# Gate and up of every f tile as one 2x2 block product, in an adaLN block with linear attention and a bilinear FFN

## The chip, the cores and the metric

One core of a Trainium2 chip. The metric is the device time of one execution in microseconds; a kernel's time is the median of its runs. All data is float32; matrix products run on float32r halves (below).

## The reference

```python
mod = (silu(c) @ w_mod).reshape(c.shape[0], 6, 1, -1)
sa, ca, ga, sb, cb, gb = (mod[:, i] for i in range(6))
h = layernorm(x) * (1 + ca) + sa
q, k, v = heads(h @ wqkv)                       # 32 heads of 16
phi = lambda t: where(t > 0, t + 1, exp(t)) + 1e-6
kv  = einsum("bhsd,bhse->bhde", phi(k), v)
z   = einsum("bhsd->bhd", phi(k))
o   = einsum("bhqd,bhde->bhqe", phi(q), kv) / (einsum("bhqd,bhd->bhq", phi(q), z)[..., None] + 1e-6)
x = x + ga * (merge(o) @ wo)
h = layernorm(x) * (1 + cb) + sb
x = x + gb * (((h @ w_gate) * (h @ w_up)) @ w_down)
```

x is 1 x 2048 x 512, w_gate and w_up 512 x 1376, w_down 1376 x 512, wqkv 512 x 1536, wo 512 x 512.

## The kernel before

**Tiles.** The 2048 tokens are 4 chunks (`ch`) of 4 token tiles (`j`) of 128; token tile `i` is `4 ch + j`. D = 512 is 4 blocks of 128 (`k`). F = 1376 is 11 f tiles, ten of 128 columns and a last one of 96.

**Float32 by halves.** Every operand of a product is split into a rounded half h (ScalarE copy, `split`, L183) and the rest l (a subtraction, L184, on VectorE or GpSimd). A product is three matmuls: h h, h l, l h.

**Order.** The program is recorded in the order of the source, and each engine runs its own part of it in that order; engines wait for each other by semaphores alone. SBUF tiles come from one pool of 99 buffers; PSUM is two pools of four banks, `ps_acc` (`acc`) and `ps_w` (`bank`).

**Stages.**
1. Layer norm of x, the modulation columns, k and the sums over tokens (`t_tile`, `z_add`), 4 chunks; q of tiles 0 to 10 among and after them.
2. The weights of kv folded into wo: `kvps` (products of `wv` and `tt`, where `tt` are the split sums of `tacc`), `w_out`, `wp`.
3. For each token tile a y step: `turn_a` transposes phi(q) (4 matmuls, L579), `turn_h` and `turn_l` (L583, L587) make its halves, `y_a` multiplies by `wp` (12 matmuls, L609), `y_seed` (L600) puts x into the bank beforehand, `y_b` (L614) copies the sum back to x and takes the statistics of layer norm 2. Before it, phi(q) is divided by its denominator: `den_p` (L487, a product with z), `den_r` (L493, a sum over a head), `den_b` (L502, L503, an add and a reciprocal for a whole chunk), `den_c` (L510).
4. Layer norm 2 by chunks: `rstd_of` (a power on GpSimd, L236), `nmr_of`, `xhat` (L245, ScalarE), `transpose` (L252), `modulated` (L266 to L271; it also writes the result `f` to DRAM as `kept`).
5. The FFN. f tiles 8, 9 and 10 (`lone`) are computed plainly, chunk by chunk, and stand between the y steps: `gate_up(ch, f)` (L684 to L686; 24 matmuls) and `down` (L708 to L710). f tiles 0 to 7 are four `pairs`. For a pair and a side (two chunks, 0 and 1 or 2 and 3) gate is one 2x2 block product and up another: rows are the two chunks, columns the two f tiles, the inner dimension is cut into two halves of 256. Seven products in place of eight (`block`, L973; `times`, L936), with sums of left factors (`Left`: a11, s1, s2, a12, s3, a22, s4) and of weights (`Right`: b11, t1, t2, b21, t3, t4, b22; L909, L920, L923, L927, on GpSimd and ScalarE). A block is 7 x 6 = 42 matmuls on four banks (`abank` to `dbank`), and `down_pair` (L957 to L959; 24 matmuls) of the blocks before stands between its fifth and sixth product. `evac` (L671) adds to x.

The left factors of the second side are made early, in `steps` of a list that is worked off a few at a time (`trickle`, `some`), written to DRAM and read back (`fetch`) at the change of sides. In the order of the source:

```python
y_step(0, lambda: den_c(3), lambda: q_b(11))
y_step(1)
y_step(2, lambda: split_gu(f0, nc.gpsimd))
y_step(3, lambda: scale_down(f0), turn=False, seed=False)
ps12 = proj(12, wq)
...
g = gate_up(0, f0)
...
y_step(4, lambda: scale_down(f2), lambda: den_a(2, 1, on=nc.vector))
g = gate_up(0, f2)
```

Of the kernel before, what the change touches and what calls it, by code (L numbers as in the profile page):

```python
# [11 lines left out]
ALU = mybir.AluOpType  # L12
# [10 lines left out]
def tile_adaln_block(  # L23
# [25 lines left out]
    lone = list(range(8, NF))  # L49
    pairs = [(f, f + 1) for f in range(0, 8, 2)]  # L50
# [165 lines left out]
    class Norm:  # L216
        def __init__(self, tiles):
            self.tiles = tiles
            self.mv = T(small, "mv", (P, NJ, 2))
            self.n = [None] * NJ  # L220
            self.ps = [None] * KD
            self.t = [None] * KD
# [25 lines left out]
        def transpose(self, *ks):  # L248
            for k in ks:
                ps = bank()  # L250
# [253 lines left out]

    def den_c(*tiles):
# [24 lines left out]
    den_z()  # L530
    den_a(0, 0, 1, on=nc.vector)
# [17 lines left out]
    q_b(7)  # L549
    den_a(0, 2, on=nc.vector)  # L550
# [24 lines left out]
    def turn_a(i):  # L575
        tps[i] = bank()
        phi = phq.pop(i)
        for k in range(KD):
            nc.tensor.transpose(tps[i][:, k * P:(k + 1) * P], phi[:, k * P:(k + 1) * P], ident)  # L579
# [9 lines left out]
    def turn(i):  # L589
        turn_a(i)  # L590
        turn_h(i)
        turn_l(i)

    def y_seed(i, of=acc_bank):

        yps[i] = of()
        if of is bank:

            nc.tensor.matmul(yps[i], wp[0][0][:, :P], wp[0][0], start=True, stop=True)
        nc.scalar.activation(yps[i], xts[i // NJ][i % NJ], AF.Copy)  # L600

    def y_a(i):
        if i not in yps:
            y_seed(i)
        pq = pqs.pop(i)
        for k in range(KD):
            (ah, al), (bh, bl) = cut(pq, k * P, (k + 1) * P), wp[k]
            for x, y in ((ah, bh), (ah, bl), (al, bh)):
                nc.tensor.matmul(yps[i], x, y, start=False, stop=k == KD - 1 and x is al, skip_group_check=True)  # L609

    def y_b(i):
        ch, j = divmod(i, NJ)
        ps = yps.pop(i)
        nc.scalar.activation(xts[ch][j], ps, AF.Copy)  # L614
        norm2[ch].stats(j, of=ps)

    def y_step(i, *more, late=(), q=None, turn=True, seed=True):
# [3 lines left out]
        if turn and i + 1 < NT and i + 1 not in pqs:  # L621
            turn_a(i + 1)
        y_a(i)
        if i + 1 in tps:
            turn_h(i + 1)
            turn_l(i + 1)
        if i - 1 in yps:
# [3 lines left out]
        if seed and i + 1 < NT:  # L631
            y_seed(i + 1)
        for do in more:
            do()
        for do in late:
            do()

    norm2 = {}


    wf = {}

    raw_f = {}

    def load_ffn(f):
        f0, n = fts[f]
        raw_f[f] = (load(wg_v[:, :, f0:f0 + n], "raw"), load(wu_v[:, :, f0:f0 + n], "raw"),
                    load(w_down[f0:f0 + n, :], "raw"))

    def scale_down(f):  # L650
        d = raw_f[f][2]
        nc.vector.tensor_tensor(d, d, gb[:d.shape[0]], op=ALU.mult)

    def split_gu(f, low=None):
        n = fts[f][1]
        wf[f] = [split_raw(raw, (P, KD, n), low) for raw in raw_f[f][:2]]

    def split_down(f, low=None):
        wf[f].append(split_raw(raw_f.pop(f)[2], low=low))

    def split_ffn(f, low=None):
        split_gu(f, low)
        split_down(f, low)

    def prepare(f):
        return lambda: (scale_down(f), split_ffn(f))

    def evac(ch, dn, js=range(NJ), last=False):
        for j in js:
            xt = xts[ch][j]  # L670
            nc.vector.tensor_tensor(xt, dn[j], xt, op=ALU.add)  # L671
            if last:
                nc.sync.dma_start(ov[ch, j], xt)

    hs = {}

    def gate_up(ch, f):

        n = fts[f][1]
        gps, ups = bank(), bank()  # L680
        for w, ps in ((wf[f][0], gps), (wf[f][1], ups)):
            for k in range(KD):
                hh, hl = norm2[ch].t[k]
# [496 lines left out]
```

## Time and profile before

| | us |
|---|---|
| median of 3 runs | 575.12 |
| lowest, highest | 574.57, 575.14 |
| span of the profiled execution | 575.5 |
| TensorE busy in it | 566.6 (98%) |
| VectorE, ScalarE, GpSimd busy | 380.3, 288.2, 158.5 |

The profiled execution is one more execution of the same program. Its span is 0.36 us above the highest of the runs; the page has no other time for it, so what lies around the span can't be told from its own rows. Busy times of matmuls overlap: a matmul is listed with the time from its start to its end, and the next begins before that end.

### The profile page before, as it was taken

The page shows a single profiled execution, that of the slowest core. Times are in us where ns is not written, and L with a number is a line of the kernel's source. Part 1 is how long each engine was busy: PE and PEld are TensorE (multiplying, and loading weights), DVE is VectorE, ACT ScalarE, POOL GpSimd, SP SyncE. Part 2 cuts the span into 40 slices and gives each one's busy share as a digit, 9 for nine tenths or more (in the row PEclk, how much of TensorE's full clock was granted, in tenths as well). Part 3 has the DMA queues.
Part 4 walks back from the last instruction along what each step waited for, and adds up shares of the span by engine and source line. Part 5 has one row for each costly group of instructions (what it writes and reads, how often), then busy time and mean ns, then how long its engine had stood idle before and what let it go on. Part 6 is the DMA issues. An engine that isn't in the chain of part 4 may idle for free.

```text
span 575.5 us, 7302 instructions
## 1 busy us (share of the span) xinstructions
PE 566.6 (98%) x2587; PEld 463.7 (81%) x2587; DVE 380.3 (66%) x628; ACT 288.2 (50%) x503; POOL 158.5 (28%) x156
## 2 busy tenths in 40 slices
PE   7999999999999999999999999999999999999997
PEld 6778888888888778878878788888888888888885
DVE  6877868868768876656377755777865354545475
ACT  3585857546366535437365535363555343534430
POOL 2000000000011300000000244676755766574610
PEclk9799999999999999999999999999999999999999
DMA  8900213401401000101705113363489826210004
GB/s 280 373 5 2 73 62 102 132 0 43 108 1 41 35 1 36 38 0 60 233 2 182 38 37 118 102 184 110 148 280 359 263 76 191 56 55 2 0 1 146
DMA packets 46500, 57.17 MB, mean 99 GB/s; under 512 B 5152, under 2 KB 23584, under 8 KB 46464
## 3 DMA queue, kind: packets, MB, share of 16 engines
q1 hardware_dynamic: 46464, 56.71, 30.5%
q8 instruction: 20, 0.33, 0.3%
q14 instruction: 16, 0.13, 0.1%
HBM read 40.96 MB, written 15.73 MB: 99 GB/s over the span
## 4 chain that ended last, share of the span: by engine, by line
PE 92%; DVE 4%; DMA 2%; ACT 1%; issue 0%; POOL 0%; SPq 0%; ACTq 0%
PE bank L941 26%; PE acc L609 7%; PE bank L198 5%; PE bank L196 5%; PE acc L959 5%; PE bank L197 5%; PE acc L957 5%; PE acc L958 5%; PE bank L685 4%; PE bank L686 4%; PE bank L684 4%; PE acc L329 3%; PE acc L328 3%; PE acc L327 3%; PE acc L709 2%; PE acc L708 2%
## 5 line engine op out<-in xcount | busy, mean ns | idle before, releaser
L941 PE MATMUL bank<-h,w 128*128 128x512 f32 x672 | 155.4, 389 | 0.1
L941 PEld LDWEIGHTS bank<-h,w 128*128 128x128 f32 x672 | 126.1, 188 | 26.7 <-DMA h<-side_s 0.5
L184 POOL TENSOR_TENSOR w<-raw,w 128x512 fp32r<-128x512 f32 x22 | 31.7, 1462 | 118.4 <-DVE mv L228 87.5
L236 POOL TENSOR_TENSOR rstd<-ve,half 128x4 f32<-128x4 f32 (+1 forms) x9 | 9.3, 1038 | 169.4 <-DVE ve L235 165.0
L671 DVE TENSOR_TENSOR x<-acc,x 128x512 f32<-128x512 f32 x80 | 50.2, 679 | 3.5 <-PE acc L959 3.5
L927 POOL TENSOR_TENSOR w<-raw,w 128x256 fp32r<-128x256 f32 (+1 forms) x28 | 33.0, 1178 | 70.2 <-ACT w L920 70.2
L947 ACT ACTIVATE bank<-bank 128x512 f32<-128x512 f32 x32 | 18.6, 582 | 66.0 <-PE bank L941 66.0
L183 ACT ACTIVATE kh<-phi 128x512 fp32r<-128x512 f32 (+1 forms) x44 | 26.9, 628 | 47.2 <-DVE phi L693 33.9
L959 PE MATMUL acc<-w,kl 128*128 128x512 f32 x128 | 49.9, 390 | 0.0
L958 PE MATMUL acc<-w,kh 128*128 128x512 f32 x128 | 49.8, 389 | 0.0
L957 PE MATMUL acc<-w,kh 128*128 128x512 f32 x128 | 49.8, 389 | 0.0
L196 PE MATMUL bank<-w,h 128*128 128x512 f32 x112 | 44.9, 401 | 0.0
L198 PE MATMUL bank<-w,h 128*128 128x512 f32 x112 | 43.9, 392 | 0.0
L197 PE MATMUL bank<-w,h 128*128 128x512 f32 x112 | 43.6, 389 | 0.0
L1028 DVE TENSOR_TENSOR g<-bank,u 128x512 f32<-128x512 f32 x16 | 11.1, 692 | 45.5 <-PE bank L941 45.5
L184 DVE TENSOR_TENSOR kl<-phi,kh 128x512 fp32r<-128x512 f32 (+1 forms) x44 | 33.4, 771 | 9.6 <-ACT kh L183 8.8
L927 POOL TENSOR_TENSOR w<-t,w 128x512 fp32r<-128x512 f32 x28 | 38.8, 1386 | 0.0
L685 PE MATMUL bank<-h,w 128*128 128x512 f32 (+1 forms) x96 | 37.7, 393 | 0.3 <-DVE h L271 0.2
L684 PE MATMUL bank<-h,w 128*128 128x512 f32 (+1 forms) x96 | 37.8, 394 | 0.0
L686 PE MATMUL bank<-h,w 128*128 128x512 f32 (+1 forms) x96 | 37.6, 392 | 0.0
L609 PE MATMUL acc<-w,xh 128*128 128x512 f32 x112 | 35.5, 398 | 0.0
L245 ACT ACTIVATE n<-x,nmr,rstd 128x512 f32<-128x512 f32 x32 | 24.0, 804 | 22.4 <-DVE nmr L239 22.4
(172 smaller groups left out, 1193.7 us busy)
## 6 DMA issues: line engine op xcount, KB each, us to landing
raw<-in_w_mod_dram SPq DMA_DIRECT2D x24, 256.0 KB, 3.8
raw<-in_B_w_down_dram SPq DMA_DIRECT2D x18, 256.0 KB, 3.7
x<-in_A_x_dram SPq DMA_DIRECT2D x16, 256.0 KB, 5.4
kept<-f SPq DMA_DIRECT2D x16, 256.0 KB, 2.0
f<-kept SPq DMA_DIRECT2D x16, 256.0 KB, 4.7
raw<-in_B_w_gate_dram SPq DMA_DIRECT2D x32, 128.0 KB, 3.2
raw<-in_B_w_up_dram SPq DMA_DIRECT2D x32, 128.0 KB, 3.4
side_s<-h SPq DMA_DIRECT2D x16, 256.0 KB, 2.9
```

Of the source, the lines that this page charges most:

```text
L184: (low or nc.vector).tensor_tensor(l, src, f32(h), op=ALU.subtract)
L196: nc.tensor.matmul(ps, ah, bh, start=i == 0, stop=False)
L197: nc.tensor.matmul(ps, ah, bl, start=False, stop=False)
L198: nc.tensor.matmul(ps, al, bh, start=False, stop=i == n - 1)
L609: nc.tensor.matmul(yps[i], x, y, start=False, stop=k == KD - 1 and x is al, skip_group_check=True)
L684: nc.tensor.matmul(ps[:n], w[0][:, k], hh, start=k == 0, stop=False)
L685: nc.tensor.matmul(ps[:n], w[0][:, k], hl, start=False, stop=False)
L927: sub = lambda out, x, y: (on or nc.gpsimd).tensor_tensor(out, x, f32(y), op=ALU.subtract)
L941: mm = lambda x, y, **kw: nc.tensor.matmul(ps, x[:, k], y, skip_group_check=True, **kw)
L957: nc.tensor.matmul(dn[j], hh[:, a:b], dh, start=i == 0, stop=False)
L958: nc.tensor.matmul(dn[j], hh[:, a:b], dl, start=False, stop=False)
L959: nc.tensor.matmul(dn[j], hl[:, a:b], dh, start=False, stop=i == len(hs) - 1)
```

## The change

- There are no `lone` tiles, and `gate_up`, `split_gu`, `modulated` for layer norm 2 and their weights are gone. Each of the 11 f tiles is a block of its own, on each side: 22 blocks. The columns of its 2x2 product are gate and up of that f tile (`Right` loads both), so one block gives gate and up for two chunks, and their product: c11 and c12 for the first chunk, c22 and c21 for the second.
- `down` takes the f tiles in groups of two (the last of three), as `fillers` that lie between the fifth and the sixth product of later blocks; the last group's stand behind the last block.
- The y steps 0 to 11 stand in a row. Products q 12 to 15 lie in steps 4, 7, 9 and 11. y 12 to 15 lie inside blocks 0 to 2 (`early`), layer norm 2 of chunks 2 and 3 in blocks 0 to 5.
- Denominators: the product with z (`den_q`, from tile 4 on) is on GpSimd; sum, add and reciprocal are done tile by tile (`den_t`) on VectorE.
- Left factors of the first side are made from tiles that stay in SBUF (`plain`), all seven of them split; only chunks 2 and 3 go to DRAM. x of chunks 2 and 3 is loaded a second time (`reload_x`).
- A y product that no `y_seed` began opens its bank itself and is added to x on VectorE.

The core of the diff:

```diff
-    lone = list(range(8, NF))
-    pairs = [(f, f + 1) for f in range(0, 8, 2)]
...
+    def den_t(*tiles):
+        for i in tiles:
+            ch, j = divmod(i, NJ)
+            den_r(ch, j)
+            d = dens[ch][:, j]
+            nc.vector.tensor_tensor(d, d, den0, op=ALU.add)
+            nc.vector.reciprocal(d, d)
+
+    def den_q(*tiles):
+        for i in tiles:
+            den_p(*divmod(i, NJ))
...
     den_z()
+    den_p(1, 0, 1)
     den_a(0, 0, 1, on=nc.vector)
...
+    den_p(1, 2)
     den_a(0, 2, on=nc.vector)
...
+    def y_step(i, q=None, pe=(), after=(), pre=(), mid=()):
         if q is not None:
             ps = proj(q, wq)
+        if i + 1 < NT:
             turn_a(i + 1)
+        run(pre)
+        run(pe)
+        if i + 2 < NT:
+            den_c(i + 2)
         y_a(i)
+        if i + 1 < NT:
             turn_h(i + 1)
             turn_l(i + 1)
+        run(mid)
+        if i > 0:
             y_b(i - 1)
         if q is not None:
             q_a(q, ps)
+        if i + 1 < NT:
             y_seed(i + 1)
+        if q is not None:
+            q_b(q)
+        run(after)
...
+            for kh in range(2):
+                t = B("raw", (P, 2, KH, self.n))
+                for i, v in enumerate((wg_v, wu_v)):
+                    nc.sync.dma_start(t[:, i], v[:, kh * KH:(kh + 1) * KH, f0:f0 + self.n])
...
+        times(c, A["s3"], R["t3"], False)
+        u3 = B("u")
+        copy(u3[:n], c)
+        c22 = B("g")
+        nc.vector.tensor_tensor(c22[:n], d, u3[:n], op=ALU.add)
+        also("s3")
+        also("pe")
+        times(c, A["a22"], R["t4"], False)
+        also("mid")
+        times(d, A["s4"], R["b22"], False)
+        c12 = B("g")
+        def rest():
+            nc.vector.tensor_tensor(c12[:n], d, u2[:n], op=ALU.add)
+            product_of(0, g[:n], c12[:n])
+        product_of(1, c, c22[:n])
+        rest()
+        also("s4")
...
+    turn_a(0)
+    ps = proj(11, wq)
+    turn_h(0)
+    turn_l(0)
+    y_seed(0)
+    den_c(1)
+    q_a(11, ps)
+    q_b(10)
+    right_load(0)
+    right_load(1)
+    y_step(0, after=[lambda: q_b(11), lambda: den_q(7), lambda: den_t(4, 5), lambda: right_sums(0)])
+    y_step(1, after=[lambda: den_q(8), lambda: den_t(6, 7)])
+    y_step(2, after=[lambda: right_split(0), lambda: den_t(8)])
+    y_step(3, after=[lambda: n2[0].rstd_of(0, 3), lambda: den_q(9, 10)])
+    reload_x(8, 9, 10, 11)
+    y_step(4, q=12, pre=[lambda: n2[0].nmr_of(0, 3)], after=[lambda: n2[0].rstd_of(3, 4), lambda: n2[0].xhat(0, 1, 2), lambda: den_t(9), lambda: n2[0].nmr_of(3, 4), lambda: den_q(11)])
+    y_step(5, pre=[lambda: n2[0].xhat(3)], after=[lambda: den_t(10), lambda: den_q(12)])
+    y_step(6, pe=[lambda: ln2_turn(0, 0, 1)], after=[lambda: ln2_f(0, 0, 1), lambda: den_t(11)])
...
+    y_step(9, q=14, pre=[lambda: n2[1].xhat(3)], pe=[lambda: ln2_turn(1, 0, 2)], mid=[lambda: ln2_f(1, 0, 2)],
+           after=[lambda: [L[k].split("a11") for k in range(KH)], lambda: L[0].sum("s1"), lambda: den_t(13)])
+    y_step(10, pe=[lambda: ln2_turn(1, 1, 3)], mid=[lambda: ln2_f(1, 1, 3)],
+           after=[lambda: right_sums(1), lambda: den_q(14), lambda: L[1].sum("s1"), lambda: L[0].split("s1"), lambda: L[0].sum("s2")])
+    y_step(11, q=15, mid=[lambda: L[1].split("s1"), lambda: L[1].sum("s2")],
+           after=[lambda: L[0].split("s2"), lambda: L[0].split("a12"), lambda: den_t(14), lambda: n2[2].rstd_of(0, 3)])
+    L[0].sum("s3", "s4", on=nc.gpsimd)
+    y_b(11)
+    L[1].split("s2", "a12")
+    L[1].sum("s3", "s4")
...
+    groups = [[0, 1], [2, 3], [4, 5], [6, 7], [8, 9, 10]]
+    order = [(s, g, f) for s in range(2) for g in range(len(groups)) for f in groups[g]]
...
+    early = {
+        (0, "a11"): [lambda: y_a(12)],
+        (0, "s1"): [lambda: L[0].split("s3"), lambda: turned(13), lambda: ln2_r(2, 3, 4)],
+        (0, "s2"): [lambda: L[1].split("s3")],
+        (0, "s3"): [lambda: [L[k].split("a22") for k in range(KH)]],
+        (0, "pe"): [lambda: y_a(13), lambda: [L[k].split("s4") for k in range(KH)], lambda: y_b(12)],
+        (0, "mid"): [lambda: den_q(15), lambda: den_c(14), lambda: ln2_m(2), lambda: ln2_x(2, 0)],
+        (0, "s4"): [lambda: y_b(13), lambda: ln2_x(2, 1)],
+        (1, "s1"): [lambda: turned(14), lambda: ln2_x(2, 2)],
...
+    for n, (s, g, f) in enumerate(order):
...
+        if s == 0 and n > 5:
+            at["s1"].append(lambda: some(3))
+        if s == 0 and n >= 5:
+            at["s4"].append(lambda: some(3))
```

580 lines of the change are left out of this document (206 added, 374 removed).

## The prediction

> **What bounds the kernel now.** I read the page first, then the waits of TensorE, then the chain in order of time, and last the groups by form, the windows and the timelines around the part that changes.
>
> ```profile
> span 575.5 us, 7302 instructions
> PE 566.6 (98%) x2587; PEld 463.7 (81%) x2587; DVE 380.3 (66%) x628; ACT 288.2 (50%) x503; POOL 158.5 (28%) x156
> ...
> PEclk9799999999999999999999999999999999999999
> ```
> ```profile
> PE acc L143 <- DVE w L138: 2.0, 1, 2.0
> ...
> PE bank L579 <- DVE xl L587: 0.6, 2, 0.3
> ...
> PE bank L685 <- DVE h L271: 0.2, 1, 0.2
> ```
>
> TensorE works 566.6 of 575.5 us, and its waits after the first stage are 0.6 + 0.2 us. So time can be won only by taking matmuls away, and every wait that the new order makes is lost in full. What is one matmul worth? The groups say 389 ns each, but they overlap; the chain gives the distance:
>
> ```profile
> 377.74 9.52 PE bank L941 x42
> 392.70 9.52 PE bank L941 x42
> ```
> ```profile
> L941 PE MATMUL bank<-h,w 128*128 128x512 f32 x672 | 155.4, 389 | 0.1
> ...
> L684 PE MATMUL bank<-h,w 128*96 128x512 f32 x32 | 12.6, 393 | 0.0
> ```
>
> 42 matmuls take 9.52 us, 0.227 us each, not 0.389. The 14.96 us to the next row hold 24 down matmuls more: 66 in 14.96, the same 0.227. The f tile of 96 columns costs as much as a full one (393 against 389 ns), so it saves like the others.
>
> **What is removed.** A plain f tile costs 24 gate/up matmuls for each of 4 chunks, 96; as a block product 42 for each of 2 sides, 84. Three tiles save 3 x 12 = 36. The two matmuls that seeded a y product in a `bank` go too. 38 x 0.227 = 8.6 us, all on the path. Transposes, q, y and down keep their number, and the last product still ends in one VectorE add and a store: nothing for the tail. With nothing new in the way the profiled time becomes 575.5 - 8.6 = 566.9. The span is 0.4 above the median of the runs, 575.12, so I take the difference and set it against the median: 566.5.
>
> **What is added: where TensorE may wait.** The plain products used to lie between the y steps, and their matmuls covered VectorE. Now y steps 0 to 11 stand in a row, with the four q products among them.
>
> ```profile
> 158.00:176.00 18.00, 18.00 (x86) 14.86 (x86) 12.57 (x24) 9.97 (x20) 3.50 (x3) 1.00 0.01 1
> ...
> 323.00:435.00 112.00, 112.00 (x496) 92.68 (x495) 75.91 (x102) 54.87 (x104) 64.84 (x58) 1.00 0.43 138
> 435.00:455.00 20.00, 19.93 (x89) 16.20 (x88) 7.23 (x11) 9.53 (x19) 15.04 (x14) 1.00 0.99 336
> ```
> (After the length: busy time of PE, PEld, DVE, ACT, POOL, the clock, the DMA share.) In the y part VectorE is busy 12.57 of 18 us, 70%, and GpSimd 3.50. The change takes the products of the denominators to GpSimd and keeps on VectorE, per tile, a reduction, an add and a reciprocal. The rows for a y step:
>
> ```profile
> 159.30 0.68 DVE L510 SCALAR_TENSOR_TENSOR h<-h,den 128x512 f32<-128x512 f32 x1
> 159.90 0.68 DVE L587 TENSOR_TENSOR xl<-bank,xh 128x512 fp32r<-128x512 f32 x1
> 160.50 0.68 DVE L510 SCALAR_TENSOR_TENSOR h<-h,den 128x512 f32<-128x512 f32 x1
> ...
> 165.66 0.69 DVE L227 BATCH_NORM_STATS2 st<-acc 128x6 f32<-128x512 f32 x1
> 166.38 0.18 DVE L228 BATCH_NORM_AGGREGATE mv<-st 128x2 f32<-128x6 f32 x1
> ```
> ```profile
> L503 DVE RECIPROCAL den<-den 128x128 f32<-128x128 f32 x4 | 3.8, 953 | 0.1
> ```
> ```profile
> L152 DVE RECIPROCAL ce<-ce x1: 177/177/177, 7.0 to 7.0; 128x4 f32<-128x4 f32 x1
> ```
> ```profile
> 160.60 0.60 PE L579 MATMUL bank<-ident,h 128*128 128x128 f32 x4
> 160.96 0.71 PE L609 MATMUL acc<-w,xh 128*128 128x512 f32 x2
> ```
> ```profile
> 161.43 0.63 ACT L292 ACTIVATE h<-h 128x512 f32<-128x512 f32 x1
> ```
>
> Starts lie 0.60 us apart for a full-width operation, 0.72 before one that needs its result. A denominator: 0.72 for the reduction, about 0.2 for an add of 32 columns, and 0.35 for the reciprocal (estimate between 177 ns for 4 columns and 953 for 128): 1.25 us. Any y step: `den_c` 0.60, `turn_l` 0.60, statistics 0.85, so 2.05. TensorE: 0.36 for four transposes (160.60 to 160.96) and 12 x 0.227 = 2.72, so 3.08. One denominator per step nearly fits (3.3 against 3.08, and four steps have a q product of 2.72 more), two do not. Place by place:
>
> *Start.* `den_c(1)` now stands behind `turn_l(0)`, where the row of 160.50 stood. It ends at 161.2; the transposes of tile 1 want it at 160.60. Loss 0.6 us; nothing lies between to hide it.
>
> *Steps 0 to 3.* Before `y_a(3)` VectorE does, from `turn_l(1)` on, which waits for ScalarE's copy (0.6) behind the row of 161.43, so from 162.65: q's sum 0.6, four denominators 5.0, one statistics 0.85, `turn_l` 1 to 3 and `den_c` 3 and 4, 3.0: 172.1. TensorE, with y_a(0) at 161.56 and 3.08 a step, wants to begin `y_a(3)` at 170.8. Loss 1.3 us. The q product of step 4 then lets VectorE catch up.
>
> *Steps 4 to 8.* The new thing is a wait: `nmr` waits on VectorE for GpSimd's power, and behind it in the queue stand `den_c` and `turn_l`, for which the next y product waits. A q product or the transposes of chunk 0 cover it: 0, unless GpSimd is in the way (below).
>
> *Steps 9 to 11 and block 0.* The seven left factors are now all split, from two chunks: 14 splits and 8 sums.
> ```profile
> 229.66 0.87 PE bank L252 x8
> ```
> ```profile
> 181.69 1.45 ACT L266 ACTIVATE f<-bank,col,col 128x512 f32<-128x512 f32 x2
> ```
> ```profile
> L614 ACT ACTIVATE x<-acc 128x512 f32<-128x512 f32 x14 | 8.3, 593 | 7.4 <-PE acc L609 7.4
> ```
> I count from the q product of step 9. TensorE, up to the second half of the fifth block product (s3): two q and four y products 16.3, four turns 1.44, the transposes of chunk 1 1.74, two seeds 0.45, 27 block matmuls 6.1: 26.1 us. VectorE begins the statistics of tile 8 after 6.2 (q product 2.72, transposes 0.36 + 0.87 and 0.25 to their end, two f 1.45, the copy 0.55), and then issues 23 full-width operations 13.8, four statistics 3.4, two denominators 2.5 and waits of 0.85 for ScalarE: 26.8. Loss 0.7, with `y_a(12)` inside the block as cover, and `y_a(13)` for the splits of a22 and s4; without them it would be up to 2.72 us more for each.
>
> Sum with free engines: 0.6 + 1.3 + 0 + 0.7 = 2.6 us. That is the low end, 569.1.
>
> **The unknown cost: GpSimd beside VectorE.** Rows of one operation with GpSimd idle and busy:
>
> ```profile
> 149.32 0.29 DVE L502 TENSOR_TENSOR den<-den,den 128x128 f32<-128x128 f32 x1
> ...
> 181.79 1.28 DVE L502 TENSOR_TENSOR den<-den,den 128x128 f32<-128x128 f32 x1
> ...
> 361.15 1.78 DVE L184 TENSOR_TENSOR h<-s,h 128x512 fp32r<-128x512 f32 x1
> ```
> ```profile
> 181.64 1.28 POOL L184 TENSOR_TENSOR w<-raw,w 128x512 fp32r<-128x512 f32 x1 [5.28 <-ACT w L183]
> ...
> 360.64 1.74 POOL L927 TENSOR_TENSOR w<-t,w 128x512 fp32r<-128x512 f32 x1
> ```
> ```profile
> L184 DVE TENSOR_TENSOR h<-s,h 128x512 fp32r<-128x512 f32 x16 | 12.6, 820 | 0.0
> ...
> L510 DVE SCALAR_TENSOR_TENSOR h<-h,den 128x512 f32<-128x512 f32 x16 | 11.2, 721 | 0.0
> ...
> L587 DVE TENSOR_TENSOR xl<-bank,xh 128x512 fp32r<-128x512 f32 x16 | 11.0, 686 | 12.5 <-ACT xh L583 12.5
> ```
>
> The same add took 0.29 us alone and 1.28 beside a GpSimd operation of 1.28 that had begun 0.15 earlier; a split took 1.78. Operations with a PSUM input keep their 0.69. So a VectorE operation on two SBUF tiles can wait for a whole GpSimd operation, 1.0 to 1.1 us. [...]
>
> How often does it strike? In the stretch 323 to 435 GpSimd was busy 58% of the time, and yet the mean split there is 820 ns against the 686 of L587, which reads PSUM: 0.13 each. In steps 0 to 2 GpSimd has nothing to do (its products come early, the weights wait for ScalarE's casts at the end of step 2). In the stretch from step 9 stand 20 such operations: ten splits, six sums, two `den_c`, two adds. 20 x 0.13 = 2.6 us by the means. By the worst rows it is more.
> ```profile
> 141.93 0.28 PE L196 MATMUL bank<-w,w 128*128 128x128 f32 x1
> 142.11 0.33 PE L197 MATMUL bank<-w,w 128*128 128x128 f32 x1
> ```
> Here TensorE already waits 0.07 us (0.18 between starts, not 0.11) for the weights of kv, and two moved products now block VectorE ahead of them: 0.6. Step 3: 0.5. Steps 4 to 6, where after each power GpSimd begins a product of 1.28 just when VectorE wants `nmr` and then `den_c`: 3.1. Block 0, where GpSimd splits the second weights beside VectorE's last splits: five operations, 5. Blocks 6 to 9, with up to six steps of the second side in each: 3. Together 12.2 us, an estimate from the 1.0 and 1.1 above. I take the means, 2.6, since they come from 16 operations and the worst rows from single ones.
>
> The loads of the second side take the same room as before: the row 435 to 455 has DMA at 0.99 and TensorE idle 0.07 us, and they are issued a block earlier now; half as many tiles are written out and read back. Nothing for it.
>
> Sum: -8.6 + 2.6 + 2.6 = -3.4 us; 575.1 - 3.4 = **571.7**.
>
> **Rivals.**
> *All of it is won:* the waits at the start and in steps 0 to 3 hide in TensorE's queue, 566.5 to 569. For it: 98% today, with the same engines. Against: the sums above do not close. Chance 0.13.
> *GpSimd eats the gain (slower):* each power or product on GpSimd holds VectorE for a whole operation at the places named. Price 2.6 + 12.2 = 14.8, so 581.3 with everything, and slower from the point where lost time passes 8.6 us, that is where the contention costs more than 6.0, half of the worst. For it: the 1.28 and 1.78 us rows, and the order of the queues. Against: the means. Chance 0.28 for slower, and 0.10 that it just about cancels.
> *A colder clock (slower):* if block 0 makes TensorE stand for some us, its clock falls.
> ```profile
> 0.00:22.00 22.00, 18.26 (x73) 14.54 (x74) 15.96 (x38) 9.95 (x15) 3.44 (x15) 0.86 0.90 317
> ```
> ```profile
> L143 PE MATMUL acc<-w 128*128 128x512 f32 x37 | 13.4, 514 | 2.0 <-DVE w L138 2.0
> ```
> The only stretch in which TensorE stood for long (22.00 less 18.26, 3.7 us) has a clock of 0.86, and matmuls of 514 ns there. [...] By the rows, if as many as those 37 matmuls ran so again, 37 x 0.227 x (514 / 389 - 1) = 2.7 us, on top of a stall of some 4: with the 2.6 and 2.6 above, 578.4. No stall in my sum is that long. Chance 0.04.
> That the change does not do what it says has no room: the count of matmuls is fixed by the loops.
>
> **The numbers.** What this kernel's measurement can tell from no change is about 0.2%, 1.15 us. Forecast (losses of 3 to 7.4 us) 0.45, and all won 0.13: faster 0.58. Same 0.10. Slower 0.28 + 0.04 = 0.32. The range: from 567.0, a little above all won, to 579.5, most of the way to the worst rows; the likeliest case's own is 569 to 574.
>
> **What would show it.** In the changed profile: 2,549 matmuls; 42 block matmuls still in 9.5 us; TensorE's waits, near nothing today, as a few us on `turn_l`, `den_c` and the splits of the left side; their place in the four step groups above and block 0; `den_c`, the 32-column adds and the splits at about 0.8 us in the mean. I am wrong if TensorE's waits sum to under 2 or over 8.6 us, if they lie in blocks 2 to 21 and not before, if they are on DMA, or if the clock leaves 1.00 after the first 22 us.

## The result and the profile after

| | before | after |
|---|---|---|
| median, us | 575.13 (4 runs, 574.57 to 577.37) | **582.53** (4 runs, 580.87 to 582.83) |
| ratio | 1 | 1.0111, 95% interval 1.0082 to 1.0139 |
| span of the profiled execution | 575.5 | 580.8 (its time: 582.47) |

The kernel became 7.4 us slower; I had forecast 3.4 us faster, with a range to 579.5. In all the results that give both numbers, a run's time is 1.7 to 1.8 us above its span. The profiled execution of before therefore took some 577.2 us, more than its median: it ran at half clock from 15.9 to 22.8 us (the 0.86 of the prediction's row for 0 to 22 us), and that of after did not (1.00 there). So the two spans differ by less than the medians.

The head of the page after, and the chain in order of time:

```profile
span 580.8 us, 7362 instructions
...
PE 563.6 (97%) x2549; PEld 457.6 (79%) x2549; DVE 376.3 (65%) x622; ACT 294.2 (51%) x530; POOL 236.1 (41%) x237
...
PEclk9999999999998998999999999999999999999999
```
```profile
270.67 9.52 PE bank L780 x42
```

2,549 matmuls, 38 fewer, and 42 block matmuls in 9.52 us: the saving is there in full. It is lost again in waits. TensorE's waits from 130 us on (total, times, longest):

```profile
PE bank L591 <- DVE h L520: 2.9, 3, 1.9
PE bank L780 <- DVE h L182: 2.5, 4, 1.3
PE acc L859 <- POOL w L182: 2.5, 1, 2.5
PE bank L780 <- DVE g L841: 1.5, 1, 1.5
PE bank L780 <- ACT bank L786: 0.2, 1, 0.2
```

The view counts a wait from the modelled end of the matmul before; by the distance of starts (less 0.227 us for a full matmul, 0.09 for a transpose, excesses over 0.12 us only) these are 13.5 us, where before has 3.4. And three stretches have half the clock. Here each is shown with the stretch ahead of it (length; busy time of PE, PEld, DVE, ACT, POOL; clock; DMA share; GB/s):

```profile
181.11:184.52 3.41, 1.49 (x10) 1.01 (x9) 2.76 (x4) 1.18 (x2) 2.18 (x2) 1.00 0.00 0
184.52:187.94 3.42, 3.42 (x15) 3.03 (x14) 3.17 (x8) 3.42 (x8) 0.00 (x0) 0.50 0.02 5
225.48:228.90 3.42, 1.84 (x6) 0.67 (x4) 3.42 (x6) 2.77 (x7) 0.93 (x2) 1.00 0.00 0
228.90:232.31 3.41, 3.16 (x8) 2.49 (x9) 1.47 (x3) 3.13 (x7) 3.41 (x4) 0.50 0.00 0
...
358.60:362.02 3.42, 0.97 (x4) 0.84 (x5) 1.86 (x4) 3.27 (x7) 3.42 (x3) 1.00 0.81 285
362.02:365.43 3.41, 3.41 (x9) 2.64 (x9) 0.00 (x0) 0.11 (x1) 3.38 (x3) 0.50 1.06 405
```

Together they cost 4.8 us in distances of starts. The balance from 130 us on: -8.6 for the matmuls, +10.1 for the waits, +1.1 in excesses below 0.12 us, +4.8 for the clock: +7.4, the difference of the medians.

Two of the waits in their engines' rows. First step 6, VectorE, GpSimd and TensorE:

```profile
176.27 1.25 DVE L237 SCALAR_TENSOR_TENSOR nmr<-mv,rstd 128x3 f32<-128x3 f32 x1 [0.96 <-POOL rstd L234]
...
180.80 1.31 DVE L508 TENSOR_TENSOR den<-den,den 128x32 f32<-128x32 f32 x1
...
182.42 0.88 DVE L237 SCALAR_TENSOR_TENSOR nmr<-mv,rstd 128x1 f32<-128x1 f32 x1
183.23 0.68 DVE L520 SCALAR_TENSOR_TENSOR h<-h,den 128x512 f32<-128x512 f32 x1
```
```profile
176.20 3.07 POOL L485 TENSOR_TENSOR f<-h,zb 128x512 f32<-128x512 f32 x2
180.25 0.55 POOL L234 TENSOR_TENSOR rstd<-ve,half 128x1 f32<-128x1 f32 x1 [0.98 <-DVE ve L233]
180.77 2.52 POOL L485 TENSOR_TENSOR f<-h,zb 128x512 f32<-128x512 f32 x2
```
```profile
184.05 0.65 PE L591 MATMUL bank<-ident,h 128*128 128x128 f32 x4 [1.92 <-DVE h L520]
```

GpSimd ends a power and begins a product of a denominator; in that moment VectorE wants an add of 32 columns, and takes 1.31 us for it. `nmr` at 176.27, which the power has just released, meets the product of 176.20 in the same way. `den_c` of tile 7 (183.23) stands behind, and TensorE waits 2.08 us by starts. In block 0 VectorE's splits do the same beside GpSimd's low halves of the second weights:

```profile
231.64 3.30 DVE L182 TENSOR_TENSOR h<-f,h 128x512 fp32r<-128x512 f32 x2
234.87 2.91 DVE L182 TENSOR_TENSOR h<-s,h 128x512 fp32r<-128x512 f32 x2
```

Two splits take 1.29 us where nothing is in the way (e13 below). Last block 8, ScalarE, VectorE and GpSimd:

```profile
348.95 1.68 ACT L181 ACTIVATE h<-s 128x512 fp32r<-128x512 f32 x3 [3.27 <-DMA side_a<-h]
```
```profile
357.59 3.40 POOL L182 TENSOR_TENSOR w<-raw,w 128x512 fp32r<-128x512 f32 x1 [4.24 <-ACT w L181]
```

The low half of a down weight, 1.28 us in the prediction's row of 181.64, takes 3.40 us, and the down product waits 2.66 us by starts. ScalarE had waited for a store of the second side before. VectorE's split that starts after it is not stretched:

```profile
357.98 0.68 DVE L182 TENSOR_TENSOR h<-s,h 128x512 fp32r<-128x512 f32 x1
```

It can also come out the other way. e3 (below) leaves block 8 as it is. There the same low half starts as far behind the scaling of its weight, 1.42 us, but it gets through in 1.60 us, and the split is the one that is held:

```profile
355.94 1.60 POOL L182 TENSOR_TENSOR w<-raw,w 128x512 fp32r<-128x512 f32 x1 [4.24 <-ACT w L181]
```
```profile
356.32 1.76 DVE L182 TENSOR_TENSOR h<-s,h 128x512 fp32r<-128x512 f32 x1
```

The stall in block 8 is 0.84 us then. So 1.8 of the 2.66 us are the collision, and the rest is a low half that starts late, because the scaling stands behind VectorE's run of operations.

### The profile page after: what moved, and what is told of

The parts are those of the page before. It is cut to its first block, busy times and chain, and to the rows that moved or that the text cites. A ratio compares the mean times of both kernels' runs of the same rounds, so it can differ in the third digit from the quotient of the medians.

```text
span 580.8 us, 7362 instructions
## 1 busy us (share of the span) xinstructions
PE 563.6 (97%) x2549; PEld 457.6 (79%) x2549; DVE 376.3 (65%) x622; ACT 294.2 (51%) x530; POOL 236.1 (41%) x237
## 4 chain that ended last, share of the span: by engine, by line
PE 78%; DVE 12%; DMA 5%; ACT 2%; POOL 1%; issue 1%; SPq 1%; DVEq 0%; POOLq 0%
PE bank L780 31%; PE acc L859 7%; PE acc L860 7%; PE acc L858 7%; PE bank L196 5%; PE bank L194 5%; PE bank L195 5%; DVE h L182 3%; PE acc L616 2%; PE acc L327 2%; PE acc L325 2%; PE acc L326 2%; DMA h<-side_s 2%; DMA raw<-in_A_wqkv_dram 2%; PE bank L250 1%; DVE h L520 1%
## 5 line engine op out<-in xcount | busy, mean ns | idle before, releaser
L780 PE MATMUL bank<-h,w 128*128 128x512 f32 (+1 forms) x924 | 219.2, 392 | 4.5 <-DVE h L182 2.5
L780 PEld LDWEIGHTS bank<-h,w 128*128 128x128 f32 (+1 forms) x924 | 170.2, 186 | 46.8 <-DVE h L182 4.6
L786 ACT ACTIVATE bank<-bank 128x512 f32<-128x512 f32 (+1 forms) x44 | 25.6, 581 | 143.6 <-PE bank L780 143.5
L182 POOL TENSOR_TENSOR w<-raw,w 128x512 fp32r<-128x512 f32 (+1 forms) x22 | 36.8, 1675 | 116.0 <-ACT w L181 116.0
L859 PE MATMUL acc<-w,kh 128*128 128x512 f32 (+1 forms) x176 | 69.3, 394 | 2.5 <-POOL w L182 2.5
L858 PE MATMUL acc<-w,kh 128*128 128x512 f32 (+1 forms) x176 | 69.3, 394 | 0.0
L860 PE MATMUL acc<-w,kl 128*128 128x512 f32 (+1 forms) x176 | 69.2, 393 | 0.0
L766 POOL TENSOR_TENSOR w<-raw,w 128x256 fp32r<-128x256 f32 (+3 forms) x44 | 45.0, 1023 | 38.2 <-ACT w L759 38.1
L766 POOL TENSOR_TENSOR w<-t,w 128x512 fp32r<-128x512 f32 (+1 forms) x44 | 57.9, 1317 | 0.0
L859 PEld LDWEIGHTS acc<-w,kh 128*128 128x128 f32 (+1 forms) x176 | 33.5, 190 | 10.0 <-POOL w L182 2.9
L858 PEld LDWEIGHTS acc<-w,kh 128*128 128x128 f32 (+1 forms) x176 | 33.5, 190 | 7.3
L860 PEld LDWEIGHTS acc<-w,kl 128*128 128x128 f32 (+1 forms) x176 | 33.3, 189 | 7.1
```

The lines of the kernel that those rows point to most:

```text
L182: (low or nc.vector).tensor_tensor(l, src, f32(h), op=ALU.subtract)
L766: sub = lambda out, x, y: (on or nc.gpsimd).tensor_tensor(out, x, f32(y), op=ALU.subtract)
L780: mm = lambda x, y, **kw: nc.tensor.matmul(ps, x[:, k], y, skip_group_check=True, **kw)
L786: nc.scalar.activation(out, x, AF.Copy)
L858: nc.tensor.matmul(dn[j], hh[:n, a:b], dh[:n], start=i == 0, stop=False)
L859: nc.tensor.matmul(dn[j], hh[:n, a:b], dl[:n], start=False, stop=False)
```

## The experiments

The theory: VectorE and GpSimd hold each other up at three places (step 6, block 0, blocks 6 to 9), and a wait of about 2 us brings 3.4 us of half clock on top. The rivals: VectorE has simply too much to do there; the stores of the second side are the cause in blocks 6 to 9; the half clock comes with the load. Ratios are to the kernel before on the same chip; line numbers in an experiment can lie a few lines off.

### e1: work for nobody

```diff
     def turn_a(i, of=bank):
         tps[i] = of()
+        if i == 7:
+            fill(tps[i], 9)      # matmuls whose result is overwritten
...
+        also("ahead")            # block 0: fill(yps[13], 8)
         times(c, A["s3"], R["t3"], False)
...
         dn = {j: acc_bank() for j in js}
+        fill(dn[js[0]], 12)      # first down product of block 8 only
```

> Adds 29 matmuls of 128x512 whose results nobody uses, in front of three of TensorE's long waits: 9 ahead of the transposes in step 6 (wait 2.08 us), 8 ahead of the s3 product of block 0 (0.38 and 1.59), 12 ahead of the first down product of block 8 (2.66). At 0.2267 us each they are 6.57 us of TensorE work for 6.3 us of waiting. Theory (the three stretches at half clock, 3.41 us long and 4.8 us dear together, are set off by TensorE's idle time): TensorE has no gap over 0.5 us at these three places, the half-clock stretches behind them go, and the kernel with more work is faster, 582.5 - 4.8 + 0.3 = 578.0. Rival (the half-clock stretches come with the load, whatever TensorE does): they stay, 582.8. Second rival (the waits' releasers are late because TensorE's own work is their input, so that matmuls ahead delay them too): the waits stay behind the added matmuls, 582.5 + 6.6 = 589 with the stretches, 584 without.

Measured: 580.12 us, ratio 1.008 (1.006 to 1.010). With 29 matmuls more it is 2.4 us faster than the changed kernel. The stretches of the three places:

```profile
181.11:187.94 6.83, 6.65 (x36) 5.34 (x35) 5.93 (x11) 4.53 (x10) 2.43 (x2) 1.00 0.01 2
225.48:232.31 6.83, 6.53 (x28) 4.60 (x26) 5.28 (x9) 6.52 (x13) 4.73 (x5) 1.00 0.00 0
358.00:366.00 8.00, 8.00 (x37) 6.63 (x36) 1.39 (x3) 2.91 (x6) 7.92 (x9) 1.00 1.02 346
```

The clock is 1.00 in all three; the profiled execution has a span of 577.5 against 580.8. Only one of the six runs (580.91) is longer than the shortest of the changed kernel (580.87). The half clock comes of TensorE's idle time, and both rivals fall. I had expected 578.0. In the profile all waits together fell from 13.5 to 8.0 us, by less than the 6.6 us of added matmuls (block 0 still has two of 0.9), and four of the six runs show a mean clock of 0.994 to 0.996, so they had half clock somewhere.

### e2: step 6

```diff
-    ... lambda: den_q(9, 10)]) ... lambda: den_q(11)]) ... lambda: den_q(12)])
+    ... lambda: den_q(9, 10, on=nc.vector)]) ...   # 11 and 12 alike
```

> Puts the four denominator products of tiles 9 to 12, in steps 3 to 5, on VectorE, where GpSimd had them: 2.4 us more work on VectorE (4 x 0.6), 6 us less on GpSimd. Theory (VectorE's rows of 1.25, 1.31 and 0.88 us behind GpSimd's 3.07 and 2.52 us are the collision of the two engines): these rows fall to about 0.2 us, VectorE comes to the scaling of tile 7 some 1.4 us earlier in spite of the added work, the wait of step 6 falls from 2.08 to about 0.6 us, and without a wait of 2 us the half-clock stretch behind it (1.67 us) goes: 582.5 - 1.4 - 1.7 = 579.4. Rival (VectorE simply has too much to do in steps 3 to 6): the added 2.4 us come on top, the wait grows to about 4.5 us, 585.

Measured: 576.93 us (574.40 to 582.28), ratio 1.003 (1.000 to 1.006). The same three operations of VectorE, with its own product between:

```profile
179.01 0.16 DVE L237 SCALAR_TENSOR_TENSOR nmr<-mv,rstd 128x3 f32<-128x3 f32 x1
...
182.46 0.19 DVE L508 TENSOR_TENSOR den<-den,den 128x32 f32<-128x32 f32 x1
...
182.96 0.10 DVE L237 SCALAR_TENSOR_TENSOR nmr<-mv,rstd 128x1 f32<-128x1 f32 x1
```

1.25, 1.31 and 0.88 us became 0.16, 0.19 and 0.10. TensorE has no wait at step 6 any more, although VectorE does four products more. In step 6 the wait was collision, all of it. The gain is larger than expected, by 2.5 us. A part of it is block 8, where GpSimd's low half got through in 1.59 us: the stall is 0.85 us, with 1.89 us elsewhere in blocks 6 to 9, and the half clock of 1.56 us behind it is gone. The rest is not explained.

### e3: block 0 on VectorE

```diff
-    L[0].sum("s3", "s4", on=nc.gpsimd)
     y_b(11)
     L[1].split("s2", "a12")
-    L[1].sum("s3", "s4")
+    for k in range(KH): L[k].sum("s3")      # s4 of both at (0, "s2")
...
-            at["s2"].append(lambda: right_split(1))
+            at["s2"].append(lambda: right_split(1, nc.vector))
...
-    den_q(15)
+    den_p(3, 3, on=nc.vector)
```

> Puts what GpSimd does during block 0 on VectorE: the two left sums s3 and s4 of k = 0 (put behind the splits of s2 and a12), the four low halves of the second right side, and the denominator product of tile 15: 3.9 us more work for VectorE, 9 us less for GpSimd; the sums for block 2 stay on GpSimd at the block's end. Theory (collision): VectorE's rows of 1.79, 1.77, 3.30 for two and 2.91 for two fall to 0.6 to 0.68 us an operation, 6.2 us back for 3.9 us added; TensorE's waits in block 0 and at the head of block 1 fall from 5.5 to about 3 us, and the half-clock stretch at 228.9 (1.57 us) goes: 582.5 - 2.5 - 1.6 = 578.4. Rival (VectorE's own work is what is late in block 0): 3.9 us come on top, 586.4.

Measured: 577.75 us, ratio 1.0047 (1.0031 to 1.0063), a little better than forecast, but not in the way forecast: block 0's waits fell from 5.5 to 4.35 us only, and the longest is new.

```profile
234.20 0.98 PE L780 MATMUL bank<-h,w 128*128 128x512 f32 x3 [1.98 <-DVE h L182]
```

The lows, now in VectorE's queue, stand ahead of the splits of a22, and two of them are still stretched (1.23 and 1.22 us) beside GpSimd's sums for block 2, which had stayed there. The gain over that is the half-clock window behind block 0, and again a shorter stall in block 8 (0.84) with no half clock behind it.

### e4: a weight scaled sooner

```diff
-        at["s4"] += [lambda n=n: right_sums(n + 2), lambda d=raw_d[s, f]: scale_down(d)]
+        at["s4"] += [lambda n=n: right_sums(n + 2)]
...
+        at["s4"].append(lambda d=raw_d[s, f]: scale_down(d))   # ahead of some(3)
```

> Scaling of a down weight ahead of the trickled jobs of a block's end, where it stood behind them on VectorE; nothing else is moved. In block 8 it comes 1.8 us earlier, GpSimd's low half of that weight can begin at about 355.8 where it began at 357.59. Theory (GpSimd's low half of 3.40 us, late and stretched beside VectorE's run of operations, is the stall of 2.66 us in block 8): it ends by 357.6 to 359.3, the stall falls to 0 to 0.9 us, and the half-clock stretch behind it (1.56 us) goes: 578.3 to 579.5. Rival (GpSimd's operation does not come through before VectorE's run pauses at 360.5, whenever it begins): its row grows to about 4.6 us, the stall stays at 2.7 us, 582.5.

Measured: 584.36 us, ratio 1.0154 (1.0131 to 1.0177). A miss for both: the stall at the down product fell to 0.71 us, and longer ones appeared.

```profile
PE bank L780 <- DVE g L832: 4.4, 2, 2.9
```

VectorE's add for c22 is late, behind splits that lie beside GpSimd's low halves and are stretched (2.89 us for two). The longer of the two waits is 3.08 us by starts, more than any in the changed kernel, and yet the clock stayed at 1.00:

```profile
377.20:380.62 3.42, 1.86 (x9) 1.21 (x7) 3.42 (x3) 0.00 (x0) 3.42 (x3) 1.00 0.65 249
380.62:384.03 3.41, 2.05 (x9) 1.62 (x10) 2.35 (x4) 0.00 (x0) 3.33 (x5) 1.00 0.93 313
384.03:387.44 3.41, 3.41 (x17) 2.35 (x16) 3.38 (x7) 1.64 (x3) 0.09 (x1) 1.00 0.86 250
```

These bounds lie on the grid of the half-clock windows of the same execution (last section): 1.71 us of the wait lie in one window and 1.36 in the next.

### e5: the second side spread out

```diff
+        def early(self, n):              # a11, a12: one job in each of
+            self.split(n)                # (3,s1) (3,s4) (4,s1) (4,s4)
+            self.f.pop(n)
...
-            at["s1"].append(lambda: some(3))
+            at["s1"].append(lambda: some(2))      # s4 alike
```

> Changes only how the second side's splits and stores are spread: the four splits of a11 and a12 go into blocks 3 and 4, one at a time, and the rest goes two at a time where it went three at a time (20 jobs from block 5 to the first point of block 10). Steps and block 0 stay as they are. Theory (in blocks 6 to 9 the stores queue up, 8.97 us from issue for four of them, ScalarE's splits wait 3.3 and 3.4 us for them, VectorE's splits come in one run behind it, and GpSimd's low half of a down weight is stretched to 3.40 us beside that run): ScalarE's two waits for stores go, the stall of 2.66 us in block 8 falls under 0.5 us, and the half-clock stretch behind it (1.56 us) goes: 582.5 - 2.3 - 1.6 = 578.6. Rival (the stall belongs to the collision alone, whatever the stores do): it stays near 2.7 us, 582.5.

Measured: 596.24 us, ratio 1.0364 (1.033 to 1.0398). The stall in block 8 fell to 0.23 us, as the theory had it, but I had made two others, 4.94 us in block 4 and 9.98 at the head of block 11:

```profile
ACT h L181 <- DMA f<-kept: 9.1, 2, 6.8
...
DVE g L845 <- DMA side_s<-h: 11.1, 1, 11.1
```

A split in the same job as its load waited for that load, 6.8 us in the longer case; and stores that come after the loads of the new side in SyncE's queue landed so late that the buffers they hold stopped VectorE for 11.1 us. That the stores are behind the stall in block 8 is not shown: the edit spreads VectorE's splits together with the stores, and GpSimd's low half got through there in 1.62 us, as in e2 and e3, which have the stores where they were.

### e6 and e7: three places at once, and the lows out of block 0

```diff
+    # e6: e2, e3's left sums, e5's trickle, and from block 0 to block 1:
+    (1, "a11"): [lambda: den_q(15), lambda: right_sums(2)],
+    # e7: e6, and
+    y_step(7, ... lambda: right_sums(1)])      # was in step 10
+    y_step(8, ... lambda: right_split(1)])     # was in block 0
```

> All three places at once. Steps 3 to 5: the denominator products of tiles 9 to 12 on VectorE, as in the run before. Block 0: the left sums on VectorE behind the splits of s2 and a12, and the denominator product of tile 15 and the four sums for block 2 moved from block 0 into block 1; the low halves of the second right side stay on GpSimd. Blocks 3 to 10: the splits of the second side spread as in the slow trickle. Theory (three separate places, each a wait and a half-clock stretch, which add up): step 6 gives 2.1 + 1.7, blocks 6 to 9 give 2.7 + 1.6, block 0's waits fall from 5.5 to about 3 and its half-clock stretch goes: 582.5 - 3.8 - 4.3 - 4.1 = 570.3, below the kernel before (575.1). Rival (VectorE is short of time from step 4 to block 1 as a whole, and what is taken away at one place comes late at the next): 575 or more, with waits of over 5 us in blocks 0 and 1.

> The kernel of the three places, with one thing more: the second right side's sums move from step 10 to step 7 and its high and low halves from block 0 to step 8, so that GpSimd has next to nothing to do in block 0. Theory (block 0's remaining waits are GpSimd's low halves beside VectorE's splits): block 0's waits fall to about 1.5 us, VectorE has time to spare in steps 8 and 9, 570.3 - 1.5 = 568.8. Rival (in steps 8 to 10 the same four operations of GpSimd cost VectorE 1.1 us each, and a step's transposes wait for it): 1.5 us less in block 0, up to 4.4 us more in steps 8 to 10, 573.

Measured: 592.06 us (ratio 1.0289, 1.0259 to 1.0319) and 589.41 (1.0237, 1.0208 to 1.0266), far above what I had forecast. Both carry the trickle's two waits (14.2 us each). Between them only the second right side moves, and VectorE's splits of a22 and s4, first e6, then e7, show what it did:

```profile
227.25 2.86 DVE L182 TENSOR_TENSOR h<-f,h 128x512 fp32r<-128x512 f32 x2
230.04 3.45 DVE L182 TENSOR_TENSOR h<-s,h 128x512 fp32r<-128x512 f32 x2
```
```profile
225.94 2.80 DVE L182 TENSOR_TENSOR h<-f,h 128x512 fp32r<-128x512 f32 x2
228.67 2.35 DVE L182 TENSOR_TENSOR h<-s,h 128x512 fp32r<-128x512 f32 x2
```

Block 0's waits are 6.0 us in e6 and 2.55 in e7, and steps 8 to 10 gained only one wait of 0.30: the lows cost 3.5 us in block 0 and next to nothing elsewhere. But the rows of e7 are still about twice 1.29. GpSimd had not left block 0:

```profile
225.75 1.31 POOL L485 TENSOR_TENSOR f<-h,zb 128x512 f32<-128x512 f32 x1
227.00 1.19 POOL L752 TENSOR_TENSOR t<-raw 128x256 f32<-128x256 f32 x1
```

These are the product and the sums that I had "moved to block 1". With nothing ahead of them in the queue they ran straight after the power before them, at 225.75 and 227.00 us, beside VectorE's splits.

### e8 to e12: putting it together

```diff
+    # e8: the changed kernel, blocks 5 to 9 only
+        dve = nc.vector if 5 <= n <= 9 else None   # lows of right_split, split_down
+    # e9: e7 with the trickle of the changed kernel
+    # e10: e9 and e8
+    # e11: e10, den_t(7) from step 1 to 2, den_t(8) from step 2 to 3
+    # e12: e11, down products of blocks 6 and 8 behind a22
+            at["mid" if n in (6, 8) else "pe"].append(...)
```

> The changed kernel with one thing altered: in blocks 5 to 9 the low halves of the next right side (4 operations) and of the down weight (1) are VectorE's, where GpSimd had them: per block some 2.7 us more work for VectorE (in its trace an operation of 128x512 takes 0.60 us in a run), 6 to 8 us less for GpSimd. Steps and block 0 stay. Theory (the stall of 2.66 us in block 8 and its half-clock stretch come of GpSimd and VectorE stretching one another): the stall falls under 0.5 us: 582.5 - 2.2 - 1.6 = 578.7. Rival (in these blocks ScalarE's waits for the side stores set VectorE's time, not GpSimd): VectorE, with more to do behind the same waits, lets TensorE wait for c22 and the splits, the sum of waits in blocks 6 to 9 stays at 2.7 us or grows by up to 2.7 us: 582.5 to 585.

> The kernel with the lows early, with the splits of the second side trickled as in the changed kernel again: so only steps 3 to 8 and blocks 0 and 1 differ from it. In the run before, the spread trickle made two waits of its own (4.81 us in block 4, for a load issued in the same job as its split, and 9.44 us at the head of block 11, for stores that come after the loads in SyncE's queue), with 3.7 us of half clock behind them. Theory (these come of the trickle alone): a span of 585.8 - 4.8 - 9.4 - 3.7 = 567.9, and blocks 6 to 9 as in the kernel with the denominators on VectorE (0.85 + 1.89 us) and 0.44 at the side change: 571.1, a time of 572.8. Rival (the waits move: what steps and block 0 give back is lost in blocks 2 to 9, since their work is only put off): 576 or more.

> The kernel of the last entry and the altered blocks 5 to 9 of the first one together. Theory (three separate places that add up): waits of blocks 6 to 9 under 0.5 us and no half-clock stretch after the first 25 us: 572.8 - 2.3 = 570.5. Rival as in the first entry (side stores): no gain on the last entry, 572.8 to 575.

> The kernel of the last entry with the denominator sums of tiles 7 and 8 one step later each (tile 7 from step 1 to step 2, tile 8 from step 2 to step 3). Theory: the wait of 0.85 us before the transposes of step 3 is VectorE's queue of step 1, and goes: 570.5 - 0.8 = 569.7. Rival (the step behind takes it over, a sum of 1.2 us that comes later): the wait turns up in steps 4 to 6, 570.5.

> The kernel of the last entry, with the down products of blocks 6 and 8 issued behind the a22 product instead of ahead of it: 6 matmuls, 1.36 us, later. In the profile of that kernel VectorE has 12 operations of 0.6 us in one run, 345.3 to 353.7, before the low half that the down product of block 8 waits for, with no operation stretched and TensorE idle for 1.69 us. Theory (what is left in block 8 is no collision but the length of VectorE's queue, and a later need hides it): the waits fall from 1.69 to about 0.3 us and from 0.50 to 0: 573.5 - 1.9 = 571.6. Rival (VectorE's queue sets the block, so the wait only moves to c22 or to the head of the next block): 573.5.

| | median, us | ratio (95%) |
|---|---|---|
| e8 | 581.96 | 1.0114 (1.0101 to 1.0127) |
| e9 | 573.94 | 0.9978 (0.9959 to 0.9996) |
| e10 | 574.13 | 0.9981 (0.9972 to 0.9990) |
| e11 | 573.54 | 0.9965 (0.9953 to 0.9978) |
| e12 | 574.10 | 0.9987 (0.9972 to 1.0001) |

e9 holds what its theory said: the trickle's two waits go, nothing moves into blocks 2 to 5, and it is 8.6 us faster than the changed kernel by steps and block 0 alone; it misses the 572.8 by 1.1 us. Its profile, the longest of the twelve runs, has the stall of 2.65 us in block 8 with half clock behind it; what the other runs had there is not known. e8 and e10 come out about as the rival forecast: with no GpSimd work on the down weight the stall in block 8 is 1.69 us, between the 0.84 and the 2.66 us of its two outcomes above, and 0.50 is new in block 6; the median gains nothing that can be told. e10 and e11 stay 3.6 and 3.8 us above their forecasts. e11 shows why block 8 still waits. VectorE's rows ahead of the low half (353.10), with none of them stretched:

```profile
345.29 2.48 DVE L865 TENSOR_TENSOR x<-acc,x 128x512 f32<-128x512 f32 x4
347.68 1.89 DVE L182 TENSOR_TENSOR h<-s,h 128x512 fp32r<-128x512 f32 x3
349.49 0.69 DVE L875 TENSOR_TENSOR raw<-raw,row 128x512 f32<-128x512 f32 x1
350.09 1.28 DVE L182 TENSOR_TENSOR kl<-phi,kh 128x512 fp32r<-128x512 f32 x2
351.29 0.69 DVE L182 TENSOR_TENSOR h<-s,h 128x512 fp32r<-128x512 f32 x1
351.89 1.29 DVE L182 TENSOR_TENSOR h<-f,h 128x512 fp32r<-128x512 f32 x2
353.10 0.69 DVE L182 TENSOR_TENSOR w<-raw,w 128x512 fp32r<-128x512 f32 x1
```

Fourteen operations in a row (I had counted 12), no gap. In e11 the 0.85 us of step 3 went, but for 0.17. In e12 the waits of blocks 6 and 8 only changed their name, as its rival had it:

```profile
PE bank L780 <- ACT u L786: 2.3, 2, 1.6
```

Issued later, the down products no longer cover ScalarE's copy of u3, for which a22 waits.

### e13 and e14: what was still open

```diff
+    # e13: e11, and in block 1 on VectorE
+    (1, "a11"): [lambda: den_q(15, on=nc.vector), lambda: right_sums(2, nc.vector)],
+    # e14: e13, and
-            at["s2"].insert(0, ... split_down(...))
+            at["s1" if 6 <= n <= 9 else "s2"].insert(0, ... split_down(...))
```

> The kernel with the sums of tiles 7 and 8 later, and the last of GpSimd's work in block 0 given to VectorE, in block 1: the denominator product of tile 15 and the four sums for block 2. They had been put behind block 0 in GpSimd's queue, but that queue is empty there, so it does them as soon as their inputs are there, at 225.8 to 231.6 in the profile of the kernel with the lows early, beside VectorE's splits (2.80 us for two and 2.35 for two). Theory (the 2.5 us of waits left in block 0 are still collision): the four splits take 1.29 us for two, 2.6 us less; the waits of block 0 fall to about 0.8 us: 573.5 - 1.7 = 571.8. Rival (they are VectorE's own length): the waits stay at 2.5 us, and 2 us of new work on VectorE makes block 1 wait: 573.5 to 575.

> The kernel of the last entry, with the split of the down weight ahead of the trickled splits in blocks 6 to 9, one point earlier: its low half then stands three operations further ahead in VectorE's queue, 1.8 us. Theory (the waits of 0.50 and 1.69 us in blocks 6 and 8 are that queue's order, and nothing behind it is pressed for time): they go, 571.8 - 2.2 = 569.6. Rival (as when the down products were moved behind a22: the wait turns up at the next need, ScalarE's copy for a22 or c22): 571.8.

Measured: e13 **571.88 us**, ratio 0.9928 (0.9907 to 0.9950), 0.1 from the forecast, faster than both kernels. The same four splits:

```profile
226.28 1.29 DVE L182 TENSOR_TENSOR h<-f,h 128x512 fp32r<-128x512 f32 x2
227.48 1.29 DVE L182 TENSOR_TENSOR h<-s,h 128x512 fp32r<-128x512 f32 x2
```

Block 0 waits 0.64 us now. The work that VectorE took over makes block 1 wait for 1.24 us, so the sum from 220 to 240 us is 1.9 against 2.5 in e11. With GpSimd out of the way VectorE is not short of time in block 0: of the 5.5 us 4.9 are gone, 3.65 if block 1's new wait is counted against them.

e14 is slower, 585.18 us, ratio 1.0169 (1.0138 to 1.0200): ScalarE's high half of the down weight now stands ahead of its copy of the bank, and waits for VectorE's scaling.

```profile
PE bank L780 <- ACT bank L786: 11.1, 4, 3.6
```

Three of these four waits have a half-clock window behind them. What is late in blocks 6 to 9 once GpSimd has no part in them is VectorE's queue (e8, e11); a cure was not found.

## Why the prediction was wrong, point by point

**Right:** 38 matmuls, 8.6 us, all on the path; nothing in the tail; the four places in the steps and in block 0; the mechanism (VectorE held by GpSimd, the second rival).

| place | free engines | worst rows added | measured after |
|---|---|---|---|
| weights of kv | 0 | 0.6 | 0.47 |
| start | 0.6 | | 0.49 |
| steps 0 to 3 | 1.3 | 0.5 | 0.85 |
| steps 4 to 8 | 0 | 3.1 | 2.08 |
| steps 9 to 11, block 0 | 0.7 | 5 | 5.53 |
| blocks 6 to 9 | 0 | 3 | 2.66 |
| change of sides | 0 | | 0.6 |
| half clock | 0 | | 4.8 |

**The step that failed** is "I take the means, 2.6". With the 2.6 of free engines I had 5.2 us of loss for the seven rows of waits, and they measure 12.7. (The kernel before has 3.4 us of waits by the same measure, and after 13.5 in all: 10.1 were added, and 1.1 in small excesses, for which my sum has no term.) By the worst rows it would have been 14.8. A mean of 0.13 us an operation over a stretch in which the two engines overlap by chance says nothing of a place where one engine's result starts the other: there the collision is not drawn at random. In after it came behind both powers ahead of step 6's wait, where the power releases `nmr` on VectorE, or VectorE has come to its add, in the moment that frees GpSimd for its product (1.25 us for 0.16 and 1.31 for 0.19; e2). In block 0 TensorE waits for VectorE's last four splits, so that most of what they are stretched by is lost (they take 6.2 us in the changed kernel, 2.6 in e13). I had both places and both prices in the text, and gave them the smaller weight.

**The second failure** is "No stall in my sum is that long". It set the bar for a colder clock at a stall of some 4 us, on which that rival's 578.4 us rested too. It was an estimate, and no run shows it; in after a wait of 2.08 us in step 6 was enough (below). The three windows cost 4.8 us, and my 0.04 for this rival was far too little: both rivals came together.

**Right in amount, in part by luck:** blocks 6 to 9. The 3 us stood there as contention. It is 1.8 of the 2.66 us, and in e2 and e3, which have the same block 8, the low half is held by some 0.3 us at most (1.60 for 1.28); the rest is the length of VectorE's queue, which also makes the 1.69 us of e8 and e11. What the stores have to do with it stays open.

**Wrong, small:** "Nothing for it" on the change of sides: 0.6 us, waits for `fetch`. And steps 0 to 3 cost 0.85 rather than 1.3.

**My own tests of it:** TensorE's waits are over 8.6 us, and the clock leaves 1.00 after the first 22 us: two of the conditions for "I am wrong" came true. The other two did not: the 2.66 us and the change of sides lie in blocks 2 to 21, but most of the waits lie before them, and only those at the change of sides are on DMA.

## What to carry to other kernels

Cost a collision of two engines place by place, by asking whether one engine's result releases the other at that moment; where it does, take the worst row, not the mean. Where two operations merely come close, as in block 8, expect either engine to be the one that is held (GpSimd's low half 3.40 us in after, VectorE's split 1.76 us in e3). Count what one wait triggers: here a wait of 2 us was worth 3.7, and 29 useless matmuls ahead of three waits were worth more than they cost. Moving a job back in the queue of an idle engine moved nothing: in e7 the product and the sums meant for block 1 ran at 225.75 and 227.00 us, still in block 0.

## What the runs showed of the hardware

**The half clock came in windows on a fixed grid.** In every profile with more than one, the starts of half-clock stretches lie whole multiples of 3.413 us apart (in after 184.523, 228.897 and 362.016: 13 and 39 windows), and a stretch, but for the one at the kernel's end, lasts one to three such windows (one, 3.413 us, in after; two, 6.827 us, in before). Half clock went with how much of the window before TensorE had stood idle. In the 16 profiles here, 130 us from the start and later and at full clock, 19 windows had 2.08 us (0.609 of the window) or more without a matmul, by starts and with every excess counted, and each was followed by half clock; some 40 had between 1.02 and 2.07 us (how many depends on the distance that a transpose is given), and none was. The two windows nearest the bound differ by less than such a count is good for. In after the wait of 2.08 us in step 6, in the window from 181.11 to 184.52, was enough. In e3 2.06 us of a wait lie between 230.70 and 234.11, and the clock is 1.00 from there to 237.53; 3.08 us across two windows (e4, 1.71 and 1.36) was not too much either. The grid does not start with the kernel: a line of it lies at 0.20 us after the span's start in after, by steps of 3.413 us back from 184.523, and at 2.28 us in before, back from 15.931. So a wait near 2 us cost 1.6 us more in some executions and not in others: in e5 and e8 the same wait of 2.08 us in step 6 lies across the end of a window, and no half clock follows. The spread of e2's runs fits this, 574.40 us (mean clock 0.999) to 582.28 (0.988), though some of their half clock may lie at the head, as in its profile (15.6 to 22.4 us).

**VectorE's small operations were held as long as large ones.** An add of 32 columns took 1.31 us beside GpSimd and 0.19 without, a multiplication of 3 columns 1.25 and 0.16, so 1.1 us more; a split of 128x512 took 1.76 in block 8 of e3 and 0.68 in that of after, 1.1 us more as well. And GpSimd was held too: 3.40 us for a low half that took 1.28 elsewhere. Which of the two was held was not settled by which started first: in block 8 GpSimd's low half starts 1.42 to 1.43 us behind the scaling and 0.4 us ahead of VectorE's next split in the changed kernel, e1, e2, e3 and e9 alike. In e2 and e3 it takes 1.59 and 1.60 us and the split 1.76; in the other three it takes 3.40 to 3.43 us, and three splits that start after it run through in their usual time (in after 0.68 us for one and 1.28 for the next two).
